# Attention scores in plain fp32 on four 64x64 tiles of the array, instead of split fp32r parts with 128-deep stacks

## The chip, the cores and the metric

The kernel runs on one core of a Trainium2 chip. The metric is the device time of one execution in microseconds (us); lower is better. PE is the matrix engine (TensorE), PEld its weight loads, DVE the vector engine, ACT the scalar engine, POOL GpSimd, SP the engine that issues most of the DMAs.

## The reference

Three stages follow each other. q, k and v are (4, 8, 576, 64): four batches, eight heads, 576 positions, 64 channels.

```python
q_rot, k_rot = rotate(q), rotate(k)                  # rotary embedding
scores = scale * q_rot @ k_rot.T                     # per batch and head: 576 x 576
attn = exp(scores - max) / sum
x = (attn @ v), heads side by side                   # 2304 x 512
logits = x @ phi                                     # soft mixture: 32 slots of 8 experts
slots = softmax over tokens of logits, transposed @ x; each expert: relu(slot @ w1) @ w2
y = softmax over slots of logits @ slot_out
h = max(y @ g1, y @ g2, y @ g3);  out = h @ wo       # 2304 x 768, then 2304 x 512
```

## The kernel before

**Groups and units.** Attention is done in 16 groups (`G`), each of one batch and two heads. A group has nine units (`units`, line 321): four blocks of 128 queries for each of the two heads, and one "rest" unit that holds the last 64 queries of both heads. Each unit goes through five steps, each a function: `emit_S` (scores: 128 queries x 576 keys into a PSUM tile `s`), `emit_max` (DVE takes the negative row maximum `nm`), `emit_exp` (ACT takes the exponential into `P` and adds up its rows), `emit_T` (PE transposes `P` in blocks of 128 back into the same `s`), `emit_Te` (ACT copies the transposes to `pt`; DVE does it for the rest unit). There are three `s` tiles, so three units can be under way.

Per group there are also `emit_rope` (rotary embedding on POOL), `emit_qk` (PE transposes q, k and the rest; ACT copies them out), `emit_PV` (attn @ v; two 64-column tiles of the array at a time, in two parts of 320 and 256 queries), `emit_u`, `emit_x`, `emit_xe`, `emit_lg` (logits and scaled output), `emit_den` and, once per batch, `emit_end`. Beside that, `convert` rewrites other weights a step at a time on DVE, ACT and POOL (`fill`), and `load_w` loads expert weights as SBUF comes free (`GROUPS` says how many buffers come with each release, `swap`).

**Scores.** The contraction is only 64 deep. `emit_qk` writes each of q, k and rest as a rounded fp32r part (`hi`, ACT), and `emit_lo` writes what is left (`lo`, DVE; for the rest POOL also copies to `qrest`, line 300). `emit_stack` then moves the parts by eight DMAs per group (line 306) so that `hi` and `lo` stand above each other on 128 partitions. A unit's scores are four fp32r matmuls of 288 columns (line 356), and six for the rest unit. For the first group no stacking is done; each unit has six or seven such matmuls (line 345).

**Order.** Nothing is scheduled at run time: `TIMES` gives each step of each unit a place (in units; `first` for the group before the steady state, `last` for the last group), all steps are sorted by it and emitted, and each engine runs its own instructions in that order. `warm` issues transposes of the identity that only keep PE at work.

```python
for w, f in (("S", emit_S), ("max", emit_max), ("exp", emit_exp), ("T", emit_T), ("Te", emit_Te)):
    at_(n + T[w][n % 9], f, n)
```

After attention come, in `emit_tail`, the experts (`h`, line 743, and `ops`, line 759), the folded second weights (`tq`, line 802), and the output stage (`g`, line 839, and `r`, line 899).

Of the kernel before, what the change touches and what calls it, by code (L numbers as in the profile page):

```python
# [8 lines left out]
F32 = mybir.dt.float32  # L9
# [9 lines left out]
TIMES = {'PV0': [5.348993, 8.061873, 6.615235, 8.258844, 8.42124],  # L19
# [4 lines left out]
 'den': 10.296417,  # L24
 'dveT': [0],
 'end': [17.064523, 17.838917, 18.010335, 19.317331],
 'exp': [-0.789958, -1.203109, -0.466349, -0.43051, -1.003865, -0.884311, -0.126511, -0.783919, -1.0402],
 'fill': [-7.27222, 8.978148, -2.813673, 4.332117, 2.208602, 8.754931, -1.185229, 5.749518, 2.465011, 5.925629],
 'fill0': [20.940143, 12.130696, 22.69602, 8.069947, -15.770382, 9.35443, -11.379411],
 'fillb': [2.298714, 7.398094, -1.509914, 4.305956, 8.349684],  # L30
# [3 lines left out]
           'exp': [-25.16811, -8.893717, -54.960507, -18.499471, -11.489709, -12.416459, -0.12097, -12.455631, -1.181958],  # L34
           'lok': -9.645275,
           'loq': -43.398111,
           'lor': -32.367129,
           'max': [-30.29715, -2.919995, 39.189116, -38.801289, -16.841612, -13.161108, -4.170338, -13.657708, -2.461004],
           'qkk': -21.547945,
           'qkq': -48.739925,  # L40
           'qkr': -39.331791,
           'stackk': -3.753959,
           'stackq': -9.399261},
# [3 lines left out]
 'last': {'PV1': [14.687795, 14.687995, 14.688195, 14.688395, 14.688595],  # L47
          'den': [48.774925, 23.436924],
          'end': [77.939459, 127.11754, 149.765832, 213.314062],
          'endb': [161.276159, 194.539127, 207.371372, 302.834297],  # L50
          'lg': [53.339377, 75.857657],
          'u1': [26.29293, 29.862203],
          'warm': [[57.500286, 4], [57.655604, 4], [97.595993, 4]],
          'x': [19.334479, 33.80813, 20.644614],
          'xe': [[50.325257, 74.427765], [55.76298, 144.692782], [51.744911, 129.696774]]},
 'lg': [16.042678],
 'loadqk': -20.803677,
 'loadr': -20.439111,
 'loadv': -1.959162,
 'loadw': 23.083762,  # L60
 'lok': -6.568922,
 'loq': -11.315028,
 'lor': -9.984437,
 'max': [-1.169451, -1.628205, -1.3601, -0.925198, -1.4374, -1.044348, -1.263452, -1.524493, -1.827084],
 'onact': [1, 0, 0],
 'qkk': -7.221075,
 'qkq': -11.736594,
 'qkr': -10.178017,
 'ropek': -13.709361,
 'ropeq': -16.661933,  # L70
 'roper': -12.998944,
 'stackk': -4.859931,
 'stackq': -9.047409,
 'u0': [10.018335, 10.286138],
 'u1': [11.576068, 12.311874],
# [3 lines left out]
 'x': [12.641556, 12.98053, 14.125551],  # L79
 'xe': [13.451958, 13.63023, 14.29362],  # L80
 'xr': [-18.945707, -83.812519, -13.655472, -25.850758],
# [4 lines left out]
def tile_kernel(ctx, tc, q, k, v, phi, w1, w2, g1, g2, g3, wo, rope, out):  # L86
# [23 lines left out]
    GROUPS = (10, 2, 4, 1, 3, 2, 1)  # L110
# [53 lines left out]
    qst = [(st0, st1)[i].tile([128, 2, 1024], F32R, tag=f"qst{i}", name=f"qst{i}") for i in range(2)]  # L164
    kst = [(st0, st1)[i].tile([128, 1152 if i else 1216], F32R, tag=f"kst{i}", name=f"kst{i}") for i in range(2)]
# [45 lines left out]
    qkt = st0.tile([128, 2, 2, 640], F32R, tag="qkt", name="qkt")  # L211
    qrest = st0.tile([128, 2, 128], F32R, tag="qrest", name="qrest")
# [33 lines left out]
    def emit_qk(g, what):  # L246

        if g == 0 and what != "q":
            ps = (ps_u.tile([128, 512], F32, tag="u", name="tk0") if what == "k" else
                  ps_s.tile([128, 2, 512], F32, tag="s", name="tr0")[:, 0])  # L250
        else:
            ps = ps_m.tile([128, 512], F32, tag="m", name=f"tq{g}{what}")
        if what == "r":
            nc.tensor.transpose(ps[:, 0:128], rot[:, 8].rearrange("p h d -> p (h d)"), ident)

            if g == 0:
                hi = kst[0][:, 0:640].rearrange("p (u c) -> p u c", c=64)[:, 0:10:9]
                nc.scalar.copy(out=hi, in_=ps[:, 64:128].unsqueeze(1).to_broadcast([128, 2, 64]))
                split[g, what, 2] = ps[:, 64:128], hi[:, 0], kst[0][:, 1152:1216]
                for x in range(2):  # L260
                    a = slice(64 * x, 64 * x + 64)
                    hi, lo = (qrest[a, z, 64 - 64 * x:128 - 64 * x] for z in range(2))
                    nc.scalar.copy(out=hi, in_=ps[a, 0:64])
                    split[g, what, x] = ps[a, 0:64], hi, lo
                return
            src = ps[:, 0:128].rearrange("p (x c) -> p x c", x=2).unsqueeze(2).to_broadcast([128, 2, 2, 64])
            hi, lo = (qkt[:, :, z, :].rearrange("p x (u c) -> p x u c", c=64)[:, :, 0:10:9, :] for z in range(2))
        else:
            i = 0 if what == "q" else 1
            for j in range(4):  # L270
                nc.tensor.transpose(ps[:, 128 * j:128 * j + 128], rot[:, 4 * i + j].rearrange("p h d -> p (h d)"), ident)
            if g == 0 and i == 0:
                for x in range(2):
                    a = slice(64 * x, 64 * x + 64)
                    hi, lo = (qst[0][a, z, 512 - 512 * x:1024 - 512 * x] for z in range(2))
                    nc.scalar.activation(out=hi, in_=ps[a], func=AF.Copy, scale=scale)
                    split[g, what, x] = ps[a], hi, lo
                return
            src = ps
            hi, lo = (kst[0][:, c:c + 512] for c in (64, 640)) if g == 0 else (qkt[:, i, z, 64:576] for z in range(2))  # L280
        if what == "q":
            nc.scalar.activation(out=hi, in_=src, func=AF.Copy, scale=scale)
        else:
            nc.scalar.copy(out=hi, in_=src)
        split[g, what] = src, hi, lo

    split = {}

    def emit_lo(g, *what):
        src, hi, lo = split.pop((g, *what))  # L290
        what = what[0]
        if what == "q":
            nc.vector.scalar_tensor_tensor(out=lo, in0=src, scalar=scale, in1=hi.bitcast(F32), op0=ALU.mult,
                                           op1=ALU.subtract)
        else:
            nc.vector.tensor_tensor(out=lo, in0=src, in1=hi.bitcast(F32), op=ALU.subtract)
        if g and what == "r":
            for x in range(2):
                a = slice(64 * x, 64 * x + 64)
                nc.gpsimd.tensor_copy(out=qrest[a, :, 64 - 64 * x:128 - 64 * x], in_=qkt.bitcast(F32)[a, 0, :, 0:64])  # L300

    def emit_stack(g, what, xs=(0, 1)):
        qs, ks = qst[g % 2], kst[g % 2]

        def move(out, in_):
            nc.sync.dma_start(out=out.bitcast(F32), in_=in_.bitcast(F32))

        for x in xs:
            a = slice(64 * x, 64 * x + 64)
            for half in range(2):  # L310
                o = slice(64 * half, 64 * half + 64)
                if what == "q":
                    c = 512 * (1 - x)
                    move(qs[o, :, c:c + 512], qkt[a, 0, :, 64:576])
                elif x == 0:
                    move(ks[o, 576:1152], qkt[a, 1, half, 64:640])
                else:
                    move(ks[o, 0:576], qkt[a, 1, half, 0:576])
# [7 lines left out]
    def emit_S(n):  # L326
        g, j = divmod(n, 9)
        x, t = units[j]
        qs, ks = qst[g % 2], kst[g % 2]
        s = ps_s.tile([128, 2, 512], F32, tag="s", name=f"s{n}")  # L330
        st[n] = s
        if g == 0:
# [764 lines left out]
```

## Time and profile before

| | |
|---|---|
| median of 3 runs | 488.08 us (487.51 to 488.62) |
| the profiled execution | 487.5 us, of which the profiled span is 485.7 us |
| PE busy | 462.3 us, 95% of the span |
| DVE busy | 341.8 us, 70% |
| ACT busy | 295.0 us, 61% |
| POOL busy | 290.1 us, 60% |
| mean granted clock of PE | 0.985 |

Attention fills the span up to about 327 us; the experts and the output stage follow. A group of instructions is shown as: line, engine, operation, out<-in, sizes, count, then busy time and mean duration of one in ns. For a column-tiled matmul "128*64" means 128 rows and 64 columns of the array. An fp32 matmul that isn't a transpose stands in the trace as two instructions, so the 8 of a `PV` step read x16. Matmuls are pipelined: the distance from one start to the next is what one costs, and its duration is longer than that.

### The profile page before, as it was taken

Reading aid. Unit: us, or ns where it says so; the run is one execution under the profiler, and the core shown is the slowest. Engines: PE = TensorE matmul, PEld = TensorE weight load, DVE = VectorE, ACT = ScalarE, POOL = GpSimd, SP = SyncE. Lnnn points to the kernel's source line nnn. Section 1 sums busy time; section 2 is a strip of 40 time slices with the busy share of each in tenths; the row PEclk is TensorE's granted clock in tenths of the full one; section 3 lists DMA queues with packets and bytes.
Section 4 is the critical chain, followed back from the end, with each engine's and each line's share of the span. In section 5 each row is a group of like instructions: output and inputs, shape, how many; then the busy total and the mean of one; then the engine's idle time right before and its main releaser. Section 6 shows DMA issues by size and latency. Waiting matters only on the chain. (4 is left out here: it accounts for less than half of the span.)

```text
span 485.7 us, 9652 instructions
## 1 busy us (share of the span) xinstructions
PE 462.3 (95%) x3336; PEld 345.7 (71%) x3336; DVE 341.8 (70%) x662; ACT 295.0 (61%) x651; POOL 290.1 (60%) x403
## 2 busy tenths in 40 slices
PE   8899999999999999999999999986999899999996
PEld 7667777787777786777777877753334677888885
DVE  7879998887998898889989897535321467545520
ACT  2688897797887977888878788640121444322311
POOL 5889889877887897697979842011000377423420
PEclk9999999999999999999999999996999999999999
DMA  7657889898989998799999757979999401111111
GB/s 212 181 146 204 219 230 249 271 253 217 282 224 263 281 255 252 214 243 286 236 248 287 186 128 219 391 241 378 329 388 410 182 1 44 66 43 65 45 65 65
DMA packets 73120, 103.19 MB, mean 212 GB/s; under 512 B 12144, under 2 KB 41456, under 8 KB 72560
## 3 DMA queue, kind: packets, MB, share of 16 engines
q1 hardware_dynamic: 73072, 102.59, 70.9%
q8 instruction: 26, 0.43, 0.4%
q14 instruction: 22, 0.18, 0.1%
HBM read 66.98 MB, written 11.01 MB: 161 GB/s over the span
## 5 line engine op out<-in xcount | busy, mean ns | idle before, releaser
L373 ACT ACTIVATE P<-s,nm 128x576 f32<-128x576 f32 x144 | 107.5, 747 | 14.9 <-DVE nm L361 12.7
L361 DVE TENSOR_REDUCE nm<-s 128x1 f32<-128x576 f32 x144 | 107.4, 747 | 9.6 <-PE s L356 6.2
L356 PE MATMUL s<-kst,qst 128*128 128x288 f32 x480 | 90.9, 312 | 3.8 <-DVE pt L413 3.8
L382 PE MATMUL s<-ident,P 128*128 128x128 f32 x576 | 89.0, 277 | 3.9 <-ACT P L373 3.8
L356 PEld LDWEIGHTS s<-kst,qst 128*128 128x128 f32 x480 | 67.7, 188 | 20.1 <-issue 7.9
L382 PEld LDWEIGHTS s<-ident,P 128*128 128x128 f32 x576 | 66.0, 141 | 20.9 <-ACT P L373 8.2
L899 PE MATMUL r<-wo,h 128*128 128x512 f32 x324 | 79.6, 396 | 0.3 <-ACT ob L863 0.2
L430 PE MATMUL u<-pt,vn 128*64 128x256 f32 (+1 forms) x512 | 76.2, 418 | 1.1 <-DVE rd L459 1.1
L899 PEld LDWEIGHTS r<-wo,h 128*128 128x128 f32 x324 | 61.1, 190 | 14.6 <-POOL h L859 0.9
L859 POOL TENSOR_TENSOR h<-hf,h 128x512 fp32r<-128x512 f32 (+1 forms) x30 | 35.4, 1180 | 42.0 <-ACT h L858 41.9
L848 DVE TENSOR_REDUCE hf<-g 128x512 f32<-128x1536 f32 (+1 forms) x26 | 40.9, 1600 | 27.6 <-PE g L839 23.5
L407 ACT COPY pt<-s 128x640 f32<-128x640 f32 x64 | 44.5, 695 | 8.0 <-PE s L384 8.0
L405 ACT COPY pt<-s 128x512 f32<-128x512 f32 x64 | 37.6, 590 | 18.2 <-PE s L382 17.6
L430 PEld LDWEIGHTS u<-pt,vn 128*64 128x64 f32 x512 | 31.0, 136 | 23.1 <-issue 9.5
L858 ACT CAST h<-hf 128x512 fp32r<-128x512 f32 (+1 forms) x30 | 17.3, 578 | 48.9 <-DVE hf L848 43.5
L623 POOL TENSOR_TENSOR raw<-raw 128x384 f32<-128x384 f32 x32 | 26.5, 828 | 19.7 <-ACT raw L621 12.7
L625 POOL TENSOR_TENSOR cv<-cv,raw 128x384 f32<-128x384 f32 x32 | 33.0, 1030 | 2.5
L711 POOL TENSOR_TENSOR wo<-wof,wo 128x512 fp32r<-128x512 f32 x6 | 7.6, 1279 | 44.7 <-ACT wo L710 44.7
L472 PE MATMUL x<-xr,ut 128*128 128x256 f32 x160 | 30.4, 305 | 0.1
L373 ACT ACTIVATION_READ_ACCUMULATOR P<-s,nm 128x1 f32 x144 | 29.0, 201 | 0.0
L440 DVE TENSOR_TENSOR ut<-u,ut 128x320 fp32r<-128x320 f32 (+1 forms) x32 | 14.5, 452 | 18.7 <-ACT ut L442 18.6
L616 DVE SCALAR_TENSOR_TENSOR cv<-raw,cv 128x384 uint32<-128x384 uint32 x32 | 24.0, 751 | 0.1
(361 smaller groups left out, 810.4 us busy)
## 6 DMA issues: line engine op xcount, KB each, us to landing
wt<-in_moe_w_dram SPq DMA_DIRECT2D x32, 1024.0 KB, 7.9
qst<-qkt SPq DMA_DIRECT2D x60, 256.0 KB, 5.5
raw<-in_moe_w_dram SPq DMA_DIRECT2D x24, 384.0 KB, 4.3
kst<-qkt SPq DMA_DIRECT2D x60, 144.0 KB, 4.1
wmd<-cv SPq DMA_DIRECT2D x24, 192.0 KB, 2.7
vn<-in_v_dram SPq DMA_DIRECT2D x16, 256.0 KB, 4.9
wm<-wmd SPq DMA_DIRECT2D x4, 1024.0 KB, 13.2
out_dram<-ob SPq DMA_DIRECT2D x16, 256.0 KB, 2.2
```

The source lines that it names most:

```text
L356: nc.tensor.matmul(s[:, h, 0:288], l, r[:, 288 * h:288 * h + 288], start=(i == 0), stop=(i == len(todo) - 1))
L361: nc.vector.tensor_reduce(out=nm[n], in_=st[n][:, :, 0:288], axis=AX.XY, op=ALU.max, negate=True)
L373: nc.scalar.activation(out=dst.rearrange("p (h c) -> p h c", h=2), in_=s[:, :, 0:288], func=AF.Exp, bias=nm.pop(n), accum_out=acc)
L382: nc.tensor.transpose(s[:, 0, 128 * c:128 * c + 128], p[:, c0 + 128 * c:c0 + 128 * c + 128], ident)
L405: copy(out=o[:, 0:4, w + q0:w + q0 + 128], in_=src[:, 0:4, :])
L407: copy(out=o[:, 0:5, q0:q0 + 128], in_=src[:, 0:5, :])
L430: nc.tensor.matmul(u[r, 0:w], vn[g][:, x, 64 * c:64 * c + 64], o[:, c, c0:c0 + w], start=(c == 0), stop=False)
L472: nc.tensor.matmul(ps[:, 256 * i:256 * i + 256], utf[:, S * z + c0:S * z + c0 + 128], xr[:, 0:hp + 2:hp + 1, :], start=(z == 0), stop=(z = ...
L625: nc.gpsimd.tensor_tensor(out=t3, in0=t3, in1=hf, op=ALU.add)
L848: nc.vector.tensor_reduce(out=h, in_=ps[:, :, 0:n].rearrange("p m n -> p n m"), axis=AX.X, op=ALU.max)
L859: nc.gpsimd.tensor_tensor(out=lo, in0=h, in1=hi.bitcast(F32), op=ALU.subtract)
L899: nc.tensor.matmul(p, a[:, s_], w, start=(z0 == 0 and z == 0), stop=(z0 == NF - 1 and z == 2))
```

## The change

The scores are computed from unsplit fp32 q and k. `emit_qk` writes them once, into `qk` (`[128, 2, 640]`, head 0 on partitions 0 to 63 and head 1 on 64 to 127). `emit_swap`, four DMAs per group, copies each head to the other half of the partitions, into `sw`. A unit is then four fp32 matmuls, one for each pair of 64 queries (column half of the array, `c`) and 288 keys (row half, `z`): each works on a 64x64 tile of its own, and the two row halves write two different PSUM banks. `emit_lo`, `emit_stack`, `qst`, `kst`, `qkt`, `qrest` and their memsets go. In the first group units 1 and 2 are computed together from `qk` alone (`both`). The table `TIMES` is another one throughout: the steps of three units now stand together. Two more weight buffers are there from the start (`GROUPS` 12 for 10), ten `warm` transposes are put between two steps of the output stage, and the `warm` entries of the last group are nine for three.

```diff
-    GROUPS = (10, 2, 4, 1, 3, 2, 1)
+    GROUPS = (12, 2, 2, 1, 3, 2, 1)
...
+        dst = qk[g % 2][:, i, 64:576]
+        if what == "q":
+            nc.scalar.activation(out=dst, in_=ps, func=AF.Copy, scale=scale)
         else:
...
+            nc.scalar.copy(out=dst, in_=ps)
+
+    def emit_swap(g, what):
+
+        i = 0 if what == "q" else 1
+        for y, cols in ((1, slice(0, 352 if i else 576)), (0, slice(352, 640) if i else slice(0, 576))):
+            a, o = (slice(64 * z, 64 * z + 64) for z in (y, 1 - y))
+            nc.sync.dma_start(out=sw[g % 2][o, i, cols], in_=qk[g % 2][a, i, cols])
...
-        if x < 2:
-            c0 = (512 if x == 0 else 0) + 128 * t
-            todo = [(qs[:, i, c0:c0 + 128], ks[:, 576 * (1 - x):576 * (1 - x) + 576]) for i in range(2)]
-        else:
-
-            todo = [(qrest[:, y, :], qkt[:, 1, z, 64:640]) for y, z in ((0, 0), (0, 1), (1, 0))]
-        for i, (l, r) in enumerate(todo):
-            for h in range(2):
-                nc.tensor.matmul(s[:, h, 0:288], l, r[:, 288 * h:288 * h + 288],
-                                 start=(i == 0), stop=(i == len(todo) - 1))
+        s = [ps_s.tile([128, 2, 512], F32, tag="s", name=f"s{n + y}") for y in range(1 + both)]
+        todo = []
+        for y, s_ in enumerate(s):
+            st[n + y] = s_
+            for c in range(2):
+                head = x + y if x < 2 else 1 - c
+                q0 = 64 + 128 * t + 64 * c if x < 2 else 0
+                for h in range(2):
+                    k0 = (0 if x + y == 1 else 64) + 288 * h
+                    z = head if both else h
+                    todo.append((h if both else 0, c, z, (qk if head == z else sw)[g % 2], q0, k0, s_, h))
+        for _, c, z, src, q0, k0, s_, h in sorted(todo, key=lambda e: e[0:3]):
+            r, o = slice(64 * z, 64 * z + 64), slice(64 * c, 64 * c + 64)
+            nc.tensor.matmul(s_[o, h, 0:288], src[r, 0, q0:q0 + 64], src[r, 1, k0:k0 + 288], start=True, stop=True,
+                             tile_position=(64 * z, 64 * c))
...
         emit_h(0, 0, (0,))
+        warm(TIMES["warmg"], ps_r, "r", True)
         stacked(4)
...
-        emit_S(1)
+        emit_S(1, True)
         emit_max(1)
         emit_exp(1)
-        emit_S(2)
         emit_max(2)
```

How the rows stand now, at the two places that matter most. PE before, in a group of the steady state, from one unit's scores over the first attn @ v part (`u_0`, split over three places) to the next group's first units (line 356 scores, 382 and 384 transposes, 430 and 433 attn @ v, 271 and 254 transposes of q, k and rest):

```order
L356 MATMUL s_1497<-kst_103,qst_101 128x288 x4
L430 MATMUL u_0_1506<-pt_4_1362,vn_1280 64x320 x2
L356 MATMUL s_1511<-kst_103,qst_101 128x288 x4
L271 MATMUL tq6q<-ident,rot 128x128 x4
L382 MATMUL s_1475<-ident,P_112 128x128 x4
L384 MATMUL s_1475<-ident,P_112 128x128
L430 MATMUL u_0_1506<-pt_4_1362,vn_1280 64x320 x2
L382 MATMUL s_1497<-ident,P_111 128x128 x4
L356 MATMUL s_1555<-qkt,qrest 128x288 x6
L254 MATMUL tq6r<-ident,rot 128x128
```

The same place of the changed program (line 290 scores, 316 and 318 transposes, 364 and 367 attn @ v): the last of three units' scores, then the whole of `u_0`, then the three units' transposes.

```order
L290 MATMUL s_1163<-qk_102 64x288
L290 MATMUL s_1163<-sw_104 64x288
L290 MATMUL s_1163<-qk_102 64x288
L290 MATMUL s_1163<-sw_104 64x288
L364 MATMUL u_0_1181<-pt_3_1044,vn_878 64x320 x8
L367 MATMUL u_0_1181<-pt_3_1044,vr 64x320 x2
L248 MATMUL tq5r<-ident,rot 128x128
L316 MATMUL s_1163<-ident,P_110 128x128 x4
L316 MATMUL s_1146<-ident,P_110 128x128 x4
L318 MATMUL s_1146<-ident,P_110 128x128
```

Where scores, attn @ v and transposes alternated unit by unit, PE now has all scores of three units and one whole attn @ v part in a piece, and all transposes of the three behind it.

ACT before, some seven units of a group (line 373 the exponential, 405 and 407 the copies of the transposes, 282 and 284 copies of q, k and rest, 621 and 597 steps of the weight conversion, 442 a part of `ut`):

```order
L373 ACTIVATE P_112,sums_1591<-s_1693,nm_1730 128x576
L405 COPY pt_5_1639<-s_1681 128x4x128
L373 ACTIVATE P_111,sums_1591<-s_1718,nm_1751 128x576
L407 COPY pt_5_1639<-s_1693 128x5x128
L405 COPY pt_5_1804<-s_1718 128x4x128
L373 ACTIVATE P_111,sums_1591<-s_1775,nm_1786 128x576
L621 ACTIVATE raw_1470<-raw_1470 128x3x128
L597 ACTIVATE cv_1823<-raw_1598 128x384
```

and in the changed program (307, then 339 and 341, 556 and 532):

```order
L307 ACTIVATE P_110,sums_1501<-s_1601,nm_1611 128x576
L307 ACTIVATE P_109,sums_1501<-s_1606,nm_1613 128x576
L307 ACTIVATE P_110,sums_1501<-s_1637,nm_1654 128x576
L339 COPY pt_5_1565<-s_1601 128x4x128
L339 COPY pt_5_1677<-s_1606 128x4x128
L341 COPY pt_5_1565<-s_1637 128x5x128
L556 ACTIVATE raw_1301<-raw_1301 128x3x128
L532 ACTIVATE cv_1697<-raw_1447 128x384
```

The same instructions stand there, three exponentials ahead of three copies.

## Rows read from the trace of the kernel before

**Rows 1.** The page: PE's busy time, and its busy tenths in 40 slices of the span.
```profile
PE 462.3 (95%) x3336; PEld 345.7 (71%) x3336; DVE 341.8 (70%) x662; ACT 295.0 (61%) x651; POOL 290.1 (60%) x403
PE   8899999999999999999999999986999899999996
```
**Rows 2.** Timeline of PE: last attn @ v step, groups 0, 9, 10, 15 (start, duration, what).
```profile
35.45 0.71 PE L433 MATMUL u<-pt,vr 128*64 128x320 f32 x4
...
208.88 0.71 PE L433 MATMUL u<-pt,vr 128*64 128x320 f32 x4
...
227.51 0.44 PE L433 MATMUL u<-pt,vr 128*64 128x320 f32 x2
...
321.29 0.71 PE L433 MATMUL u<-pt,vr 128*64 128x320 f32 x4
```
**Rows 3.** Windows: busy of PE, PEld, DVE, ACT, POOL; clock; DMA share; GB/s.
```profile
208.90:227.50 18.60, 18.27 (x141) 14.35 (x139) 17.52 (x37) 15.51 (x38) 16.41 (x26) 1.00 0.89 246
```
**Rows 4.** Timeline of PE within that group; in brackets idle time and its releaser.
```profile
211.70 0.77 PE L356 MATMUL s<-kst,qst 128*128 128x288 f32 x4 [0.33 <-DVE pt L413]
...
218.89 0.68 PE L356 MATMUL s<-kst,qst 128*128 128x288 f32 x4
219.41 0.60 PE L382 MATMUL s<-ident,P 128*128 128x128 f32 x4
219.77 0.48 PE L472 MATMUL x<-xr,ut 128*128 128x256 f32 x2
220.09 0.69 PE L356 MATMUL s<-kst,qst 128*128 128x288 f32 x4
220.71 0.76 PE L430 MATMUL u<-pt,vn 128*64 128x320 f32 x4
221.40 0.80 PE L356 MATMUL s<-kst,qst 128*128 128x288 f32 x4
222.03 0.60 PE L271 MATMUL tq12q<-ident,rot 128*128 128x128 f32 x4
...
226.38 1.30 PE L430 MATMUL u<-pt,vn 128*64 128x320 f32 x8
```
**Rows 5.** Chain of waits: fp32 matmuls on four column tiles, 512 columns each.
```profile
358.15 13.01 PE ops L759 x120
```
**Rows 6.** Lines by form on DVE and POOL: `lo` of k, of the rest, copies to `qrest`.
```profile
L296 DVE TENSOR_TENSOR qkt<-tq2k,qkt 128x512 fp32r<-128x512 f32 x1 | 0.7, 692 | 0.0
L296 DVE TENSOR_TENSOR qkt<-tq2r,qkt 128x256 fp32r<-128x256 f32 x1 | 0.4, 425 | 0.3 <-ACT qkt L284 0.3
L300 POOL CAST qrest<-qkt 64x128 fp32r<-64x128 f32 x30 | 9.0, 299 | 4.8 <-DVE qkt L296 3.8
```
**Rows 7.** The page: DMA issues, KB of one, us from issue to landing.
```profile
qst<-qkt SPq DMA_DIRECT2D x60, 256.0 KB, 5.5
kst<-qkt SPq DMA_DIRECT2D x60, 144.0 KB, 4.1
```
**Rows 8.** The page: costliest groups (busy us, mean ns, idle before).
```profile
L373 ACT ACTIVATE P<-s,nm 128x576 f32<-128x576 f32 x144 | 107.5, 747 | 14.9 <-DVE nm L361 12.7
L361 DVE TENSOR_REDUCE nm<-s 128x1 f32<-128x576 f32 x144 | 107.4, 747 | 9.6 <-PE s L356 6.2
L407 ACT COPY pt<-s 128x640 f32<-128x640 f32 x64 | 44.5, 695 | 8.0 <-PE s L384 8.0
```
**Rows 9.** Timeline of the start: PE's first scores, DVE's first maxima.
```profile
11.65 3.44 PE L345 MATMUL s<-kst,qst 128*128 128x288 f32 x19
...
13.72 2.16 DVE L361 TENSOR_REDUCE nm<-s 128x1 f32<-128x576 f32 x3
```
**Rows 10.** Windows at the end of attention, start of the experts, output stage.
```profile
331.70:339.10 7.40, 6.02 (x57) 3.27 (x57) 2.30 (x12) 0.91 (x4) 1.60 (x5) 0.50 1.04 367
339.10:341.80 2.70, 2.70 (x16) 0.73 (x20) 1.98 (x7) 0.62 (x1) 0.07 (x1) 0.50 0.90 330
386.30:389.60 3.30, 3.30 (x10) 2.46 (x9) 2.09 (x4) 1.56 (x4) 1.68 (x3) 0.50 0.00 0
```

More of the change, by code (lines that the diff above doesn't have):

```diff
@@ L46 @@
  'hact': [[2, 2], [2, 5], [2, 1], [0, 5]],
[L47 to L64, printed above, removed]
- 'onact': [1, 0, 0],
[L66 to L75, printed above, removed]
+ 'last': {'PV1': [17.889935, 17.890135, 17.890335, 17.890535, 17.890735],
+          'den': [22.629306, 27.484992],
+          'end': [129.429645, 189.213325, 199.35016, 229.989663],
+          'endb': [195.168778, 223.276502, 235.64524, 302.727101],
+          'lg': [58.274873, 110.206728],
+          'u1': [37.862833, 48.292379],
+          'warm': [[43.510374, 4], [48.645468, 4], [65.417533, 4], [84.386275, 4], [131.667341, 4], [134.737954, 4], [143.20948, 4],
+                   [167.667344, 4], [217.988062, 4]],
+          'x': [11.291267, 49.853259, 46.898819],
+          'xe': [[27.621704, 42.205763], [63.616644, 246.935738], [49.079074, 93.909442]]},
+ 'lg': [16.685218],
+ 'loadqk': -21.117445,
+ 'loadr': -26.062787,
+ 'loadv': -5.020159,
+ 'loadw': 27.731145,
+ 'max': [-0.00471, -0.928047, -1.930197, -0.414537, -0.644289, -2.363393, -0.008209, -1.02241, -2.136036],
+ 'onact': [1, 0, 0],
+ 'qkk': -7.59766,
+ 'qkq': -9.698343,
+ 'qkr': -10.970905,
+ 'ropek': -14.13953,
+ 'ropeq': -16.806381,
+ 'roper': -17.747714,
+ 'swapk': -7.090556,
+ 'swapq': -7.365792,
+ 'u0': [6.999335, 8.121391],
+ 'u1': [9.99713, 10.906705],
  'warm': [0, 0],
@@ L163, in tile_kernel @@
     rcos, rsin = rp[1][:, 0:64], rp[1][:, 64:128]
-    qst = [(st0, st1)[i].tile([128, 2, 1024], F32R, tag=f"qst{i}", name=f"qst{i}") for i in range(2)]
-    kst = [(st0, st1)[i].tile([128, 1152 if i else 1216], F32R, tag=f"kst{i}", name=f"kst{i}") for i in range(2)]
+    qk = [(st0, st1)[i].tile([128, 2, 640], F32, tag=f"qk{i}", name=f"qk{i}") for i in range(2)]
+    sw = [(st0, st1)[i].tile([128, 2, 640], F32, tag=f"sw{i}", name=f"sw{i}") for i in range(2)]
     xy = late.tile([128, 5, NP, 130], F32, tag="xy", name="xy")
@@ L254, in emit_qk @@
             nc.tensor.transpose(ps[:, 0:128], rot[:, 8].rearrange("p h d -> p (h d)"), ident)
[L256 to L265, printed above, removed]
@@ L266, in emit_qk @@
-            src = ps[:, 0:128].rearrange("p (x c) -> p x c", x=2).unsqueeze(2).to_broadcast([128, 2, 2, 64])
-            hi, lo = (qkt[:, :, z, :].rearrange("p x (u c) -> p x u c", c=64)[:, :, 0:10:9, :] for z in range(2))
-        else:
[L269 to L280, printed above, removed]
@@ L281, in emit_qk @@
-        if what == "q":
-            nc.scalar.activation(out=hi, in_=src, func=AF.Copy, scale=scale)
-        else:
[L284 to L318, printed above, removed]
+            src = ps[:, 0:128].rearrange("p (x c) -> p x c", x=2).unsqueeze(2).to_broadcast([128, 2, 2, 64])
@@ new lines, in emit_qk @@
+            nc.scalar.copy(out=qk[g % 2].rearrange("p x (u c) -> p x u c", c=64)[:, :, 0:10:9, :], in_=src)
+            return
+        i = 0 if what == "q" else 1
+        for j in range(4):
+            nc.tensor.transpose(ps[:, 128 * j:128 * j + 128], rot[:, 4 * i + j].rearrange("p h d -> p (h d)"), ident)
+        dst = qk[g % 2][:, i, 64:576]
+        if what == "q":
+            nc.scalar.activation(out=dst, in_=ps, func=AF.Copy, scale=scale)
+        else:
+            nc.scalar.copy(out=dst, in_=ps)
@@ L324, in tile_kernel, with emit_S @@
     Pt = [st2.tile([128, 1152], F32, tag=f"P{i}", name=f"P{i}") for i in range(2)]
[L326 removed]
+    def emit_S(n, both=False):
         g, j = divmod(n, 9)
         x, t = units[j]
[L329 to L332, printed above, removed]
[L335 to L357 removed]
@@ L508, in warm @@
     def warm(n, pool, tag, first):
-        w = pool.tile([128, 2, 512], F32, tag=tag, name=f"warm{tag}") if first else run["warm"]
-        run["warm"] = w
+        if first:
+            w = pool.tile([128, 512] if tag == "r" else [128, 2, 512], F32, tag=tag, name=f"warm{tag}")
+            run["warm"] = w if tag == "r" else w[:, 0]
         for _ in range(n):
-            nc.tensor.transpose(w[:, 0, 0:128], ident, ident)
+            nc.tensor.transpose(run["warm"][:, 0:128], ident, ident)
     def emit_end(b, step, t0=0, t1=5):
@@ L933, in tile_kernel @@
         emit_rope(0, "r")
-        emit_lo(0, "k")
         emit_qk(0, "q")
@@ L986, in tile_kernel @@
                     at_(z + E["qk" + w], emit_qk, g, w)
-                    at_(z + E["lo" + w], emit_lo, g, w)
                 for w in "qk":
-                    at_(z + E["stack" + w], emit_stack, g, w)
+                    at_(z + E["swap" + w], emit_swap, g, w)
                 at_(z + T["loadv"], load_v, g)
```

68 lines of the change are left out of this document (23 added, 45 removed), and 14 rows, old and new, of the table TIMES.

## The prediction

> **What bounds the kernel now.** I read the page first: PE is busy 95% of the span and only two of the 40 slices fall below eight tenths [rows 1]. Then the timeline of PE: the last attn @ v step of group 0 starts at 35.45, that of group 15 at 321.29 [rows 2], so 15 groups take 285.8 us, 19.06 each; an ordinary one, without a batch's end, takes 18.63 (208.88 to 227.51). In the window of that group PE is busy 18.27 of 18.60 us, DVE 17.52, POOL 16.41, ACT 15.51, all at full clock [rows 3]. The reader is to see there that PE sets the pace, and that the others are too near to be forgotten. Within the group the timeline shows one visible wait of PE, 0.33 us [rows 4]; with the latency behind it I take 0.5 us of waiting per group. So what the scores cost on PE counts in full, until another engine or a wait takes over.
>
> **Scores, old.** Between scores and transposes four matmuls of 288 columns take 0.52 us from start to start (218.89 to 219.41) [rows 4], 0.13 each. Eight units by four and one by six are 38 matmuls, 4.97 us a group.
>
> **Scores, new.** A unit is four fp32 matmuls on four 64x64 tiles. What fp32 costs is seen in the experts: 120 instructions take 13.01 us on four column tiles with 512 columns each [rows 5], so the eight of one step take 0.867 us, 1.69 ns per column, and the four tiles share that time in full. For 288 columns this is 0.49 us if the four new tiles also share. They are two column halves by two row halves, and no row of before has two row halves at work together. Ends: 0.49 (all four overlap, like the four column tiles) and 0.97 (only column halves overlap). I take 0.49, the nearest row: nine units then take 4.4 us, **0.6 less per group**. The Trainium skill, TensorEngine Tiling (Array Packing), "Key Properties", says that different tiles load and multiply in parallel, in 64x64 mode too; by it the sum is the one taken; for the row halves no run here shows it yet.
>
> **Going into tiles and out.** A tiled piece has a price at its ends. Into attn @ v after scores: 0.62 for the four score matmuls ahead of it (220.09 to 220.71) against 0.52, +0.10. Such a piece of four instructions of 320 columns takes 0.69 to the next start (220.71 to 221.40), where eight in a row take 1.13 (226.38 to 227.51 [rows 2, 4]), so four without ends some 0.54: +0.15; the scores after it take 0.63 (221.40 to 222.03), +0.11 [rows 4]. Together 0.36 for a round trip. Before, a group has four (`u_0` in three places, `u_1` in one): 1.44. Now it has three, one per three units, as scores and attn @ v stand in one piece twice: 1.08. New are two inner changes, from 64x64 to 128x64. Their bounds are 0 and a round trip's 0.36; I take 0.15 each, less than half. Sum: -1.44 + 1.08 + 0.30, **about 0.1 less per group**. The same page's rule, same section, is that changing the tiling mode drains the engine. The rows above agree, with some 0.1 us at each end. By the rule the inner changes would not be free and rival 1 below would fall; no row shows such a change, so it keeps its chance.
>
> **Waits.** Three units' scores now need all three `s` tiles free together, and the three exponentials stand ahead of the three copies on ACT (shown above). Worst off is the third with little beside it: scores of units 3, 5, 4, then matmuls of `x`. From its first score to the end of unit 3's scores is 0.65 (0.49 and the latency of a matmul); then a maximum 0.75 and three exponentials of 0.75 [rows 8], with 0.1 each for reading the sum: the last is done at 3.95, its five transposes at 4.5 (four of these and two of `x` take 0.68, 219.41 to 220.09 [rows 4], so 0.11 each). PE has 4.4 of work for that time: three units 1.47, ten matmuls of `x` 1.2, 13 transposes 1.4, ends 0.3. The next scores wait for unit 3's copy, which comes behind the third exponential, 3.95 + 0.7 [rows 8], and for whatever ACT has left of the third before. In the other two thirds attn @ v covers. I put waits at 0.6 to 0.8 per group for 0.5: **0.1 to 0.3 given back**.
>
> **DVE, POOL and DMA** lose work: the `lo` parts, 0.69 twice and 0.43 per group, two copies to `qrest` of 0.30 [rows 6]. That takes DVE to 15.7 and POOL to 15.8 us of the group; ACT keeps its 15.5. None is on the path now, so the gain is nothing by itself, but it is what lets PE go faster: a group of 18.0 leaves 2 us of room on each. The eight stacking DMAs, 1.6 MB a group, become four of 0.46 MB. They take 4.1 to 5.5 us to land [rows 7] and are issued seven units ahead of their use, behind no late transfer on SP's queue: nothing.
>
> **Sum per group:** -0.6 - 0.1 + 0.2 = -0.5, to -0.7 when waits stay; I take -0.6, 18.0 for 18.63. Over 15 groups **-9 us**.
>
> **First group.** Its units have six or seven matmuls, some 58 in all, 7.5 us; now 4.4. But the scores are tiled now in five separate pieces, +1.7. The first maximum starts at 13.72, though the first unit's scores (from 11.65, six matmuls, 0.8) are done by 12.6 [rows 9]: DVE has the `lo` parts first. Now it can start at 12.9, behind a pair of units of 0.97. Against that stands the wait for the first swap, landing 4 to 5.5 us after 12; the old rest unit came at 17.5, so this is about as early. Bounds -4 and +3; I take **-1.5**.
>
> **Clock.** At the end of attention the granted clock is 0.5 (the 1.2 GHz level) for 7.4 us with short DVE steps between PE's, and for the first 2.7 us of the experts, where PE is busy throughout; once more for 3.3 us in the output stage [rows 10]. In the 7.4 us PE is busy for 6.02, in between it waits for DVE. The added `warm` transposes stand in such waits; at the full level the 2.7 and the 3.3 us would halve and the 7.4 lose up to 2. Bounds 0 and -5; I take **-2.5**. They fill waits for DVE, so their own cost is nothing; without that cover the 42 added would cost 4.6 us at 0.11.
>
> **The expert weights.** DMA is saturated there (share 1.04 [rows 10]). The two more buffers take 2 MB out of that stretch, some 5 us at 367 GB/s; so the experts, which come 13 us earlier, should find their weights as now.
>
> In all -9 - 1.5 - 2.5 = -13. The profiled execution took 487.5 us, 0.6 under the median of 488.08; 474.5 on its scale, **475** on the median's.
>
> **The rivals.**
> 1. *Waits stay small and the inner changes are free:* -0.6 - 0.36 per group, -14; with the start at -3 and the clock at -4, 467. For it: all engines have room. Against: the chain above is longer than PE's work.
> 2. *The gain is eaten by waits:* DVE, ACT and PE hand over three units in a burst, and each third waits 0.2 more: no gain per group, leaving only start and clock, 484; at +0.3 per group 488, no change.
> 3. *Slower: the row halves don't run together.* The scores' place on PE, nine units a group. The point that decides: the forecast gains 0.6 per group, and start and clock 0.27 more (4.0 over 15); nine units use that up at 0.10 each, so above 0.59 us a unit the change loses. At 0.97 a group gains 9 x 0.48 = 4.3 over the forecast, +3.7 x 15 = 56 us, and with the start +3 about 545. In between, a pair of row halves that overlaps in part, 0.63 a unit, gives +0.66 x 15, 495. For it: no row shows row halves together. Against: four column tiles share perfectly [rows 5]. The page TensorE: Matmul & The Clock Gate of the Trainium skill ("Measured speedup vs the span model") has four row tiles at 3.07 times one; taken as a rate, 0.49 x 4 / 3.07 gives that 0.63.
>
> **How the numbers follow.** Forecast case 0.56 (468 to 482), rival 1 0.20, rival 2 0.13, rival 3 0.11. Within 0.2% (some 1 us) is what a measurement of this kernel can't tell from no change. Rival 2 splits into 0.08 faster, 0.04 same, 0.01 slower. Faster: 0.56 + 0.20 + 0.08 = 0.84, less 0.02 for accidents of so long an order; same 0.04 + 0.01; slower 0.11 + 0.01 + 0.01. The range reaches from rival 1 with its bounds, 463, to rival 2, 486, and leaves out rival 3 and the far ends.
>
> **What would show it.** Right: the spacing of the last attn @ v steps at 17.7 to 18.2 in ordinary groups; eight score instructions of 64x64 within about 0.49 us, in two sets of four that start together; PE's waits on ACT's copies in the third with `x`; clock at 1.00 at the experts' start. Wrong: score instructions starting in pairs, 0.24 us apart, four times a unit (rival 3); PE idle for 0.3 us or more ahead of each three scores (rival 2); the experts waiting for weights.

## The result and the profile after

The changed kernel takes 468.15 us (median of 4 runs, 467.75 to 469.29), the kernel before 487.79 (4 runs, 485.63 to 488.62): a ratio of 0.961, 95% interval 0.957 to 0.964, or 19.6 us less. The forecast was 475 with a range of 463 to 486. The profiled execution took 469.29 us, with a span of 467.5 for 485.7.

The page's busy times, PE's slices, and the granted clock (compare [rows 1]):

```profile
PE 448.6 (96%) x3894; PEld 304.4 (65%) x3894; DVE 318.5 (68%) x609; ACT 289.6 (62%) x648; POOL 282.9 (61%) x372
PE   8698999999999999999999999998999899999996
PEclk9999999999999999999999999998999999999999
```

PE is still the engine that is always busy, 13.7 us less of it. DVE has lost 23.3 us, more than PE. Only one slice of the clock falls below nine tenths.

Now the marks by which the groups were counted, the last attn @ v step, in the timeline of PE for groups 0, 3, 4 and 15 (compare [rows 2]):

```profile
29.77 0.71 PE L367 MATMUL u<-pt,vr 128*64 128x320 f32 x4
...
84.83 0.71 PE L367 MATMUL u<-pt,vr 128*64 128x320 f32 x4
...
102.77 0.71 PE L367 MATMUL u<-pt,vr 128*64 128x320 f32 x4
...
304.78 0.71 PE L367 MATMUL u<-pt,vr 128*64 128x320 f32 x4
```

15 groups take 275.0 us, 18.33 each, for 19.06: **0.72 less per group, 10.9 in all**. Two ordinary groups in windows (columns as in [rows 3]):

```profile
67.33:84.83 17.50, 17.50 (x176) 11.71 (x173) 15.73 (x33) 15.19 (x36) 16.47 (x22) 1.00 0.58 170
84.83:102.77 17.94, 17.73 (x176) 11.86 (x174) 15.86 (x33) 15.65 (x38) 15.62 (x23) 1.00 0.66 198
```

PE is busy 17.50 of 17.50 and 17.73 of 17.94, where before it was busy 18.27 of 18.60 [rows 3]. So PE lost some 0.65 of work and 0.2 of waiting. DVE is busy 15.7 to 15.9 where it was 17.52, and the DMA share went from 0.89 to about 0.6.

The scores themselves, one unit in the timeline of PE in a row of units:

```profile
26.73 0.40 PE L290 MATMUL s<-sw 64*64 64x288 f32 x1
26.74 0.40 PE L290 MATMUL s<-qk 64*64 64x288 f32 x1
26.75 0.40 PE L290 MATMUL s<-sw 64*64 64x288 f32 x1
26.75 0.40 PE L290 MATMUL s<-qk 64*64 64x288 f32 x1
26.97 0.40 PE L290 MATMUL s<-sw 64*64 64x288 f32 x1
26.98 0.40 PE L290 MATMUL s<-qk 64*64 64x288 f32 x1
26.99 0.40 PE L290 MATMUL s<-sw 64*64 64x288 f32 x1
26.99 0.40 PE L290 MATMUL s<-qk 64*64 64x288 f32 x1
27.22 0.40 PE L290 MATMUL s<-sw 64*64 64x288 f32 x1
```

Four instructions start within 0.02 us, the next four 0.24 later, the next unit 0.49 after the first: `qk` and `sw` sit in different halves of the rows and run together in full.

Two costly groups of the page, which answer to [rows 8], and the copies to the other half, which answer to [rows 7]:

```profile
L307 ACT ACTIVATE P<-s,nm 128x576 f32<-128x576 f32 x144 | 105.4, 740 | 38.1 <-DVE nm L295 36.7
L295 DVE TENSOR_REDUCE nm<-s 128x1 f32<-128x576 f32 x144 | 101.7, 750 | 22.5 <-PE s L290 22.1
sw<-qk SPq DMA_DIRECT2D x32, 144.0 KB, 4.4
```

The work per unit is as it was; ACT and DVE now wait longer for what comes before them (38.1 for 14.9, 22.5 for 9.6). They wait, PE does not: that is the mark of PE as the bound. Between 30 and 300 us the list of PE's waits has four entries:

```profile
PE s L316 <- ACT P L307: 1.9, 4, 1.0
PE s L290 <- DVE pt L347: 0.7, 2, 0.4
PE s L290 <- ACT pt L339: 0.6, 1, 0.6
PE u L364 <- DVE lgp L423: 0.4, 1, 0.4
```

Together 3.6 us; of waits for ACT's copies, which the prediction expected in each third with `x`, there is one, of 0.6 us. The end of attention, in the timeline of PE (the `warm` transposes that follow the last `x`, and the first `h`), and that stretch with the one behind it in windows (compare [rows 10]):

```profile
311.94 0.71 PE L448 MATMUL warms<-ident 128*128 128x128 f32 x5
...
321.32 0.98 PE L678 MATMUL h<-wt,sitxr 128*32 128x512 f32 x4 [0.38 <-DVE sitxr L584]
```

```profile
311.00:321.40 10.40, 8.53 (x109) 6.61 (x111) 6.42 (x25) 0.91 (x4) 2.07 (x6) 1.00 1.05 389
321.50:324.80 3.30, 3.30 (x20) 0.84 (x16) 2.43 (x6) 0.74 (x1) 0.04 (x1) 0.50 1.05 387
```

From the end of `x` to the first `h` are 9.38 us, all at full clock, for 12.25 before (326.85 to 339.10, most of it at 0.50). The one stretch at 0.50 (1.2 GHz) now is the first 3.3 us of the experts, with PE busy throughout; the prediction had expected 1.00 there. The three other executions show a mean clock of 0.999 for 0.996 and are 1.0 to 1.5 us shorter.

**Where the 18.2 us of span went:** groups 1 to 15 give 10.9; the start, together with the last group's end, 4.0 (the end of `x` is 14.9 earlier); the end of `x` to the first `h` 2.9; all behind it 0.4. The split between the first two depends on the mark: `u_0` stands at another place in the group now, so the first mark is 5.7 earlier and the last group's end gives 1.6 back. Counted by the start of the last `x` step of each group (46.86 and 326.73 before, 43.95 and 311.82 now), the groups give 12.0 and the start 2.9.

### The profile page after: what moved, and what is told of

Read it like the earlier page. It is cut to its first block, busy times and chain, and to the rows that moved or that the text cites. A ratio compares the mean times of both kernels' runs of the same rounds, so it can differ in the third digit from the quotient of the medians.

```text
span 467.5 us, 10528 instructions
## 1 busy us (share of the span) xinstructions
PE 448.6 (96%) x3894; PEld 304.4 (65%) x3894; DVE 318.5 (68%) x609; ACT 289.6 (62%) x648; POOL 282.9 (61%) x372
## 4 chain that ended last, share of the span: by engine, by line
PE 61%; DVE 7%; ACT 3%; issue 2%; POOL 1%; ACTq 0%; DVEq 0%; POOLq 0%
PE r L835 15%; PE u L364 9%; PE s L290 8%; PE s L316 7%; PE h L678 3%; PE g L774 3%; PE ops L694 3%; PE u L367 2%; PE x L406 2%; ACT P L307 2%; DVE hf L783 2%; PE tq L737 2%; PE warms L448 1%; PE e L492 1%; PE s L318 1%
## 5 line engine op out<-in xcount | busy, mean ns | idle before, releaser
L307 ACT ACTIVATE P<-s,nm 128x576 f32<-128x576 f32 x144 | 105.4, 740 | 38.1 <-DVE nm L295 36.7
L295 DVE TENSOR_REDUCE nm<-s 128x1 f32<-128x576 f32 x144 | 101.7, 750 | 22.5 <-PE s L290 22.1
L316 PE MATMUL s<-ident,P 128*128 128x128 f32 x576 | 84.5, 278 | 5.6 <-ACT P L307 4.5
L290 PE MATMUL s<-qk 64*64 64x288 f32 x584 | 82.0, 412 | 2.3 <-ACT pt L339 1.2
L290 PE MATMUL s<-sw 64*64 64x288 f32 x568 | 81.6, 412 | 0.6 <-ACT pt L339 0.6
L316 PEld LDWEIGHTS s<-ident,P 128*128 128x128 f32 x576 | 64.0, 141 | 19.0 <-ACT P L307 15.9
L364 PE MATMUL u<-pt,vn 128*64 128x256 f32 (+1 forms) x512 | 69.6, 412 | 0.4 <-DVE lgp L423 0.4
L364 PEld LDWEIGHTS u<-pt,vn 128*64 128x64 f32 x512 | 34.1, 136 | 33.5 <-DVE nm L295 12.3
L290 PEld LDWEIGHTS s<-sw 64*64 64x64 f32 x568 | 36.1, 132 | 15.5 <-issue 4.2
L290 PEld LDWEIGHTS s<-qk 64*64 64x64 f32 x584 | 36.3, 132 | 14.5 <-ACT pt L341 5.1
L406 PE MATMUL x<-xr,ut 128*128 128x256 f32 x160 | 27.1, 299 | 0.0
```

What stands on the lines that cost most here:

```text
L290: nc.tensor.matmul(s_[o, h, 0:288], src[r, 0, q0:q0 + 64], src[r, 1, k0:k0 + 288], start=True, stop=True, tile_position=(64 * z, 64 * c))
L295: nc.vector.tensor_reduce(out=nm[n], in_=st[n][:, :, 0:288], axis=AX.XY, op=ALU.max, negate=True)
L307: nc.scalar.activation(out=dst.rearrange("p (h c) -> p h c", h=2), in_=s[:, :, 0:288], func=AF.Exp, bias=nm.pop(n), accum_out=acc)
L316: nc.tensor.transpose(s[:, 0, 128 * c:128 * c + 128], p[:, c0 + 128 * c:c0 + 128 * c + 128], ident)
L364: nc.tensor.matmul(u[r, 0:w], vn[g][:, x, 64 * c:64 * c + 64], o[:, c, c0:c0 + w], start=(c == 0), stop=False)
L406: nc.tensor.matmul(ps[:, 256 * i:256 * i + 256], utf[:, S * z + c0:S * z + c0 + 128], xr[:, 0:hp + 2:hp + 1, :], start=(z == 0), stop=(z = ...
```

## The experiments

The theory under test was that of the prediction: PE is the bound, the tiles and the grouping by threes shorten its work, the relief of the other engines is worth nothing by itself, and the start and the clock give a few us more. Every ratio is to the kernel before; "over the change" is the distance between the median and 468.15.

**1. Only column halves together.** In all units but the first pair, the four matmuls read the same half of the rows; for that the whole of k is copied for one head.

```diff
-        for y, cols in ((1, slice(0, 352 if i else 576)), (0, slice(352, 640) if i else slice(0, 576))):
+        for y, cols in ((1, slice(0, 640 if i else 576)), (0, slice(352, 640) if i else slice(0, 576))):
...
-                    z = head if both else h
-                    todo.append((h if both else 0, c, z, (qk if head == z else sw)[g % 2], q0, k0, s_, h))
+                    z = head if both else 0
+                    todo.append((h, c, z, (qk if head == z else sw)[g % 2], q0, k0, s_, h))
```

> All scores but the first pair on one row half of the array (two column tiles at a time, k copied whole). Theory, PE sets the pace and the four tiles share its time in full: a unit takes 0.97 us for 0.485, 4.4 us a group more, 468 + 66 = 534 us (524 to 542), score instructions starting in twos, 0.24 us apart. Rival, PE has room that the waits in the bursts of three hide: 490 to 515 us.

530.94 us, ratio 1.092 (1.085 to 1.099); ordinary groups take 21.58 between the marks, and over 15 groups the mean is 22.16, 3.8 over the changed kernel's. Rival 3 had 4.3 over the forecast's. The score instructions start in twos, 0.24 us apart, as rival 3 had them. So the change stands on the row halves running together.

**2. The tiles alone, in the order of before.**

```diff
-TIMES = ...
+TIMES = ...
```

The second table is that of before, with the two copies due where the stack was.

> The changed kernel with the table of places of the kernel before (units one by one, attn @ v of 320 columns in three places; the warm transposes of the last group as before too). Theory, tiled pieces have a price at their ends: a group has nine tiled pieces for three and four inner changes for two, 6 x 0.36 + 2 x 0.14 = 2.4 us a group more, so 468 + 36 = 504 us (495 to 508) and ordinary groups of 19.9 to 20.3 us. Rival, the gain is that of cheaper scores and the grouping by threes is only another order: 468 to 476 us, groups below 18.3 us.

499.95 us, ratio 1.026 (1.022 to 1.029); 19.51 in ordinary groups. The tiles in single units lose 2.6%, and the new table brings 32 us from there: 22.3 in the groups (19.82 in the mean for 18.33), 8.2 by the first mark. The time lies in the theory's range, but by luck: a group costs 1.5 more than in the changed kernel, where the theory had 2.4, and the ordinary groups are under its 19.9 to 20.3; the rest came from the start above all. The start and the end of attention hold some 10 us at half clock each. That the order by threes saves the 1.5 by the ends of the tiled pieces, up to nine a group for three, is argued from their price in [rows 4] and not shown apart: the whole table was exchanged.

**3. The low parts back.** DVE's three subtractions and POOL's two copies return, into one scratch tile that nothing reads.

```diff
+        nc.vector.tensor_tensor(out=scr, in0=ps, in1=hi, op=ALU.subtract)
+        nc.gpsimd.tensor_copy(out=scr[a, 256:384], in_=scr[a, 0:128])
```

> The changed kernel with the work of the removed lo parts put back (three subtractions per group on DVE, 1.8 us, and two copies on POOL, 0.6 us, into a scratch tile, from group 1 on; results unused). Theory, the relief of DVE and POOL is worth nothing by itself: 467 to 471 us. Rival, it is a large part of what came out better than the forecast (-0.72 us a group for -0.6): 475 us or more.

490.03 us, ratio 1.0046 (1.0028 to 1.0064): **the whole gain is gone**, and the theory falls at this point. Mixed here are DVE's time, the place of the subtraction in DVE's queue (that of q stood ahead of the maxima of the third triple, waiting for ACT's copy), POOL, and a fourth thing: the subtraction reads the PSUM tile that ACT copies from, and `ps_m` has one such buffer, which PE needs next for transposes, `x` and, at a batch's end, `e` (the kernel before holds it in the same way). The next three runs separate the first three; the last stays with DVE's time.

**4 and 5. DVE's subtractions alone, at two places.** Number 4 has the places of number 3; in number 5 the subtraction of q stands behind those maxima. The last two lines are number 4's place and number 5's.

```diff
+        nc.vector.tensor_tensor(out=lo, in0=ps, in1=hi, op=ALU.subtract)
...
-                    at_(z + E["qk" + w] + 0.4, emit_lo, g, w)
+                    at_(z + E["qk" + w] + (0.9 if w == "q" else 0.4), emit_lo, g, w)
```

> Adds to the changed kernel, per group, VectorE's three subtractions of the low parts alone (3 x some 0.6 us, result unused, one scratch tile, no GpSimd copies), at the places they had when both halves came back at once: the low part of q stands ahead of the maxima of the third triple on VectorE and waits there for ScalarE's copy of q. Theory A (the place in VectorE's queue is what counts): 478 to 490 us here and 467 to 473 us in the run with the low part of q behind those maxima. Theory B (the time on VectorE counts, wherever it stands): both runs within 3 us of each other, both over 476 us. Theory C (it was GpSimd's copies and the waits between the two engines): 467 to 471 us here.

> The same three subtractions as in the run before, but the low part of q is given 0.5 steps later and so stands behind the maxima of the third triple on VectorE. Theory A (place): 467 to 473 us, at least 5 us below the run before. Theory B (time): within 3 us of it and over 476 us.

489.96 us (1.0045, 1.0022 to 1.0068) and 490.25 us (1.0042, 1.0022 to 1.0061). The place is worth nothing; three subtractions per group, 1.8 us of DVE (0.69 twice and 0.43), cost 21.8 us in all. Windows of number 4 for the two ordinary groups shown above:

```profile
73.34:91.65 18.31, 18.14 (x175) 11.73 (x173) 17.44 (x36) 15.04 (x36) 14.70 (x21) 1.00 0.51 142
91.65:111.11 19.46, 17.99 (x176) 11.70 (x174) 17.32 (x36) 15.59 (x38) 15.74 (x23) 1.00 0.63 183
```

DVE is back at 17.4 us, what it had before [rows 3], and the groups are at 18.3 and 19.5, PE waiting 0.2 and 1.5 of it. Over 15 groups the mean is 19.38, **1.05 more**; the first mark comes at 34.47, 4.7 later, with this window at the start:

```profile
16.00:25.00 9.00, 7.42 (x37) 4.64 (x38) 4.02 (x7) 4.28 (x10) 7.57 (x12) 0.52 0.60 183
```

15 x 1.05 + 4.7 = 20.5, and the span grew by 19.9. The start runs at 0.50 from 16.4 to 30.0, so part of the 4.7 is the clock's. Two entries in the list of PE's waits between 30 and 300 us show two ways by which the groups lose:

```profile
PE s L327 <- ACT P L318: 5.2, 7, 1.2
PE e L488 <- DVE scr L270: 3.9, 3, 2.1
```

The first was 1.9 in the changed kernel: the exponentials come late, and ACT's own wait for the maxima grew from 32.6 to 49.1 us. The second is new: PE stands until the subtraction has read its PSUM tile; with four smaller entries of that kind it is 5.6 us. So with DVE at 17.4 us in this order no ordinary group came under 18.3, but how much of that is DVE's time and how much the longer hold of the one buffer, no run separates: none gives DVE this work on other data.

**6. POOL's copies alone.**

```diff
+            nc.gpsimd.tensor_copy(out=scr[a, x], in_=qk[g % 2][a, :, 0:64])
```

> Adds GpSimd's two 64x128 copies per group alone (the relief of GpSimd put back, result unused), fed from qk, with no subtraction on VectorE. Theory (this relief is worth nothing by itself): 467 to 470 us. Rival (GpSimd's delay of the sums and of the rotation reaches TensorE): 473 us or more.

471.79 us, ratio 0.966 (0.964 to 0.968), 3.6 over the change, between the ranges of the two theories. In the profiled executions the span is 2.4 longer, 0.4 by the first mark and 2.1 in the groups, and that not evenly: groups 9 to 12 lose 0.25 to 0.70 each, the other eleven are as they were within 0.03. PE shows no wait for POOL; DVE's wait for POOL's sums grew:

```profile
DVE rd L398 <- POOL sums L397: 7.7, 9, 1.9
```

It was 4.1 in the changed kernel, and 2.1 of the growth of 3.6 lies between 177 and 255 us, where those four groups are. In number 3, with DVE full, two copies of the same size cost nothing on top of number 4.

**7. Each copy twice more, into DRAM tiles of their own,** behind the two that are needed.

```diff
+        for d in extra:
+            for o, a, cols in todo:
+                nc.sync.dma_start(out=d[o, cols], in_=qk[g % 2][a, i, cols])
```

> Each copy of q and k to the other half is issued twice more, into DRAM tiles that nothing else uses, behind the two that are needed, so that no copy waits for another: some 18 MB of traffic and eight issues per group put back, about what the change took away. Theory (the relief of the transfers is worth nothing while the expert weights have twelve buffers to start in): 467 to 470 us. Rival (the traffic delays the loads and copies that the conversions and the next scores wait for, or the expert weights start later): 473 us or more.

491.9 us, ratio 1.007 (1.004 to 1.0095). The rival was right that it costs, but not evenly: some groups are unchanged (17.50 to 18.29), two lose over 4 us, four 1.3 to 2.3, and the first mark is 7.0 later; those two groups and the start each hold a stretch at half clock. The timelines of SP's queue and of ACT at the start show what is late:

```profile
15.32 1.23 SPq L268 DMA_DIRECT2D sw<-qk  x2
16.59 2.52 SPq L272 DMA_DIRECT2D ex0q<-qk  x4
19.15 3.53 SPq L524 DMA_DIRECT2D raw<-in_moe_w_out_dram  x5
...
23.88 0.54 ACT L538 ACTIVATE cv<-raw 128x384 f32<-128x384 f32 x1 [8.66 <-DMA raw<-in_moe_w_out_dram]
```

One issue takes SP 0.63 us here, with the gap behind it. Eight more per group hold it for 5, the load of `raw` is issued that much later, and ACT, which works in order, stands 8.66 us before a conversion while the exponentials wait behind it. So at the start the load left 5.0 us later, and ACT's wait ended 6.5 later than in the changed kernel (23.88 for 17.43): mostly the queue that issues. In the groups the bytes came with the issues, and this run doesn't separate them.

An earlier try at the same question issued each copy three times to the same target:

```diff
-            nc.sync.dma_start(out=sw[g % 2][o, i, cols], in_=qk[g % 2][a, i, cols])
+            for _ in range(3 if g else 1):
+                nc.sync.dma_start(out=sw[g % 2][o, i, cols], in_=qk[g % 2][a, i, cols])
```

> From group 1 on every swap DMA is issued three times (12 for 4 a group, 1.4 MB for 0.46 MB: nearly the bytes of the old stacking). Theory, the smaller DMA volume is worth nothing: within 1.5 us of 468. Rival, fewer bytes on the DMA engines make loads land sooner and shorten waits: 472 us or more.

689.32 us, ratio 1.412 (1.408 to 1.417). It says nothing of bytes: a later copy waits until the one before has landed, and everything behind it on SP's queue waits too. The list of SP's waits:

```profile
SPq L267 <- DMA sw<-qk: 247.5, 120, 7.1
```

**8. Ten buffers for the expert weights** from the start, as before, for twelve, and four with the first release for two.

```diff
-    GROUPS = (12, 2, 2, 1, 3, 2, 1)
+    GROUPS = (10, 4, 2, 1, 3, 2, 1)
```

> Ten weight buffers from the start for twelve, four at the first release for two. Theory, the experts find their weights anyway: within 1.5 us of 468. Rival, the DMAs bound the end of attention and the experts, and 2 MB more there at 390 GB/s cost 3 to 5 us: 471 to 473 us.

472.36 us, ratio 0.969 (0.967 to 0.972): 4.2 over the change; the one execution at full clock took 471.02. The rival was right. In the timeline of PE the experts wait 2.3 us for weights, and the window behind it is at half clock (the half clock at the experts' start is gone in return):

```profile
351.48 1.06 PE L694 MATMUL ops<-wt,hts 128*32 128x512 f32 x8 [0.66 <-DMA wt<-in_moe_w_dram]
354.20 1.93 PE L694 MATMUL ops<-wt,hts 128*32 128x512 f32 x8 [1.66 <-DMA wt<-in_moe_w_dram]
```

```profile
354.10:357.50 3.40, 3.30 (x15) 1.64 (x16) 0.76 (x2) 0.28 (x1) 0.00 (x0) 0.50 1.02 416
```

**9. Few warm transposes:** three fours in the last group for nine, none behind them.

```diff
-          'warm': [[43.510374, 4], [48.645468, 4], [65.417533, 4], [84.386275, 4], [131.667341, 4], [134.737954, 4], [143.20948, 4],
-                   [167.667344, 4], [217.988062, 4]],
+          'warm': [[65.417533, 4], [84.386275, 4], [131.667341, 4]],
...
- 'warmg': 10,
+ 'warmg': 0,
```

> The changed kernel with three groups of four warm transposes in the last group as before (for nine) and none in the output stage. Theory, they hold the clock: the stretch at the lower level comes back at the start of the experts and in the output stage, 470 to 472.5 us. Rival, they cost what they give: 467 to 469 us.

471.95 us (469.49 to 473.75), ratio 0.967 (0.964 to 0.971): 3.8 over the change, in the theory's range, but the trace doesn't bear the theory out. The profiled execution, one of the fastest (469.51), has a stretch at half clock at 15.6 to 22.5 us and none at the end of attention, at the experts or where the ten transposes stood:

```profile
314.00:324.00 10.00, 7.02 (x91) 3.40 (x95) 5.91 (x23) 1.42 (x5) 1.67 (x5) 1.00 1.05 388
```

There the end of `x` to the first `h` takes 9.0 us without the added transposes, for 9.4 with them. The three slowest executions (473.1 to 473.8) have mean clocks of 0.978 to 0.982 for 0.991 in the two fastest; where they lose it is not shown.

**10. Units 1 and 2 singly in the first group.**

```diff
-        emit_S(1, True)
+        emit_S(1)
...
+        emit_S(2)
```

> Units 1 and 2 of the first group one by one and so after the first swap, not as a pair before it. Theory, the pair hides the swap's landing at the start: scores start at about 15.4 for 11.8 us in the trace, 470 to 472 us. Rival, the start has slack behind it: within 1 us of 468.

472.94 us, ratio 0.970 (0.968 to 0.973): 4.8 over the change, a little more than the theory had. PE waits 3.49 us for the copy and starts the next scores at 16.10. The first mark is at 33.12 for 29.77, and the start has a stretch at half clock:

```profile
17.10:24.00 6.90, 5.69 (x32) 3.08 (x30) 4.54 (x8) 4.52 (x11) 3.34 (x4) 0.51 0.63 191
```

Run 9, whose start is that of the change, has such a stretch too, and its first mark is 1.1 later; so about that much of the 3.3 need not be the pair's.

**11. Two early conversion steps later,** for the 2.1 us that ACT waits for `raw` at the start of the changed kernel.

```diff
- 'fill0': [33.659339, 10.773146, 13.326385, 6.721487, -32.33328, 13.992392, -30.049426],
+ 'fill0': [33.659339, 10.773146, 13.326385, 6.721487, -10.2, 13.992392, -10.1],
```

> The first two steps of the weight conversion placed behind the first three units (before them, ACT waits from 15.3 to 17.4 us for a load, with a copy behind it that PE waits for). Theory, that wait is on the start's chain: 466 to 467 us. Rival, other waits take its place: within 0.7 us of 468.

469.9 us (468.78 to 471.52), ratio 0.965 (0.963 to 0.968): 1.7 over the change, so no gain, and outside both ranges. ACT's wait is gone from the trace, and the first mark comes at 29.97 for 29.77: something else sets the start.

## Why the prediction was right, and where it was not

**Scores.** Right: 0.49 per unit by the row of the experts [rows 5], seen in the timeline, and run 1 prices the other case. By the page TensorE: Matmul & The Clock Gate of the Trainium skill ("Measured speedup vs the span model"), four row tiles (of 32 rows) at 3.07 times one, taken as a rate, the unit was estimated at 0.63; the trace shows 0.49, so that rate can't be carried over to these two halves.

**Ends and inner changes.** Right in size. From scores in 64x64 to attn @ v in 128x64 the price is 0.14, where 0.15 was taken (0.33 instead of 0.24 from the last four score instructions to the next start, some 0.05 within attn @ v). Rival 1's free inner changes fell with that. The rule of the Trainium skill, TensorEngine Tiling (Array Packing), "Key Properties", is that a change of mode drains the engine; the trace agrees as far as this price goes.

**Waits.** The term that was mis-sized. The prediction put waits at 0.6 to 0.8 per group for 0.5; PE is idle for 0 and 0.2 in the two groups above, and the waits listed between 30 and 300 us come to 3.6. That makes the groups 10.9 shorter instead of 9: the first half of rival 1 (467 us) came true, the second did not. The chain that was to make the next scores wait for ACT's copy in each third with `x` is not seen; the ordinary groups (17.5 to 18.7) reach past both ends of the 17.7 to 18.2 that were named.

**DVE, POOL and DMA.** "the gain is nothing by itself, but it is what lets PE go faster": the second half is right and is more than the prediction made of it; the first half can't be kept. Runs 3 to 5 give DVE its 1.8 us back and lose 21.8, 15.8 of it in the groups in run 4, more than the 10.9 that they had gained, with no more instructions on PE. Room on DVE doesn't end at zero: at 15.8 us of 17.9 its maxima come in time for ACT and PE, at 17.4 of 18.3 to 19.5 they come late in part. The working took the chain of one third of a group with DVE free at its beginning; what DVE has left to do from the third before had no place in it, and neither had the one `ps_m` buffer that a subtraction keeps from PE. That this is how the time is lost is argued from the waits in run 4; shown is that the subtractions on DVE cost it, at either of two places in its queue. POOL's relief is worth 3.6 by the medians, 2.4 by the profiled spans (run 6). Of the transfers only the issues are shown to cost (run 7). These worths overlap and are not a sum: tiles without the new table, or both without DVE's relief, are no faster than the kernel before.

**First group.** -1.5 was forecast, with -4 as the far bound; it gives -2.9 by the last `x`, or -4.0 together with the last group's end by the marks that the prediction used. Scores start at 11.80 (11.65 before) and the first maximum at 13.05 for 13.72 [rows 9]:

```profile
13.05 1.42 DVE L295 TENSOR_REDUCE nm<-s 128x1 f32<-128x576 f32 x2 [2.28 <-PE s L290]
```

The sign was right, the size too small. The clock isn't what was missing: the start of the kernel before runs at full clock as well,

```profile
11.60:35.50 23.90, 20.41 (x145) 16.09 (x145) 18.08 (x32) 17.14 (x42) 21.17 (x30) 1.00 0.59 160
```

and so does that of the change (its line PEclk above). Which of the start's terms was mis-sized is not shown. A start at half clock is a danger all the same: the profiled executions of runs 1 to 5 and 7 to 10 hold 7 to 14 us of it there, those of runs 6 and 11 none. Run 9 changes nothing at the start, so the same start comes with and without it; what decides is not shown.

**Clock at the end.** -2.5 forecast; the end of `x` to the first `h` and all behind it give -3.3. That the added `warm` transposes brought it is not shown: run 9 has the same stretch at full clock without them, and loses 3.8 in the median elsewhere or in other executions. They are 34 in the traces (52 for 18), not 42, so their cost without cover would have been 3.7 at 0.11. **The weights:** right, by run 8, and against what I expected of that run.

**The sum.** On the profiled executions 469.29 came for 474.5: 1.9 from the groups, 2.5 from start and tail, 0.8 from the end. The other 1.7 of the 6.9 between 475 and 468.15 are how the two profiled executions stand to their medians (0.6 below before, 1.1 above after).

## What to carry to other kernels

Don't price the relief of an engine at zero because PE is hardly seen to wait for it: when that engine is busy nine tenths of a stage, put the work back into the new order and measure, and check which buffers the work holds. Small fp32 products with 64 contracted rows fill the array when the operands stand in both halves of the partitions; each change of tiling has a price, so the pieces should be long. Before a copy is called free, count its issue (here 0.63 us) among the loads behind it on the same queue. Before a time is put down to the clock, compare the granted clock of both kernels in that stretch.

## What the runs showed of the hardware

- 64x64 tiles in both row halves and both column halves run fp32 together in full: four instructions 0.24 us apart from the next four at 288 columns. With one row half alone (run 1) a group of nine units is 3.8 longer in the mean.
- At the start of run 7 four issues of copies took 2.5 us of SP's queue, 0.63 each; in the earlier try a second write to a target waited for the first one's landing (120 waits, 247.5 us), and the queue with it.
- The granted clock was 0.50 for 7 to 14 us within the first 32 us in the profiled executions of runs 1 to 5 and 7 to 10, with PE busy for 5.69 of 6.90 us of it in run 10 and for 9.99 of 10.24 in run 1, and 1.00 there in those of the kernel before, the change and runs 6 and 11. In run 9, whose start is that of the change, the first mark came 1.1 us later with it.
